# First query tile's loads: heads interleaved over the partitions, list prices and due times changed (attention and two MLPs, Trainium2)

## The chip, the cores and the metric

The kernel runs on one core of one Trainium2 chip. The metric is device time in microseconds of that core, median of the runs shown. The profiled execution is one run of its own, with a profile beside it.

## The reference

```python
def _attn_ref(q, k, v):              # (4, 8, 576, 64): batch, heads, sequence, head size
    scores = scale * np.matmul(q, k.transpose(0, 1, 3, 2))
    mask = block_i >= block_j        # blocks of 64 positions, lower block triangle
    scores = np.where(mask, scores, -1000000000.0)
    scores = scores - np.max(scores, axis=-1, keepdims=True)
    attn = np.exp(scores)
    attn = attn / (np.sum(attn, axis=-1, keepdims=True) + 1e-09)
    return np.matmul(attn, v)

x = attn_out.transpose(0, 2, 1, 3).reshape(B * S, H * D)          # 2304 x 512
h = x @ w_in;   g = s * np.maximum(h, 0) ** 2 + b;  x = g @ w_out   # 512 -> 2048 -> 512
h = x @ w2_in;  g = np.maximum(0.01 * h, h);        x = g @ w2_out  # 512 -> 2048 -> 512
```

All of it is float32. The kernel splits the operands of the large products in two fp32r parts, high and low, and adds three products for each.

## The kernel before

**Tiles.** The sequence is cut in five query tiles of 128 positions (the last has 64), for all four batches at once, so that an MLP block has 512 columns (256 in the last). `ORDER` runs them as 0, 1, 2, 4, 3. The first MLP of a block (`m_in`, lines 967 to 1008, PE line 985; `m_out`, lines 1013 to 1050, PE line 1028) goes over 16 chunks of 128 hidden units, each with 12 matmuls in and 12 out, and the attention of the next tile (`later_block`) is spread between them. The second MLP (PE lines 1235 and 1301) comes after all of it, in six steps of a product with seven terms, one for each quadrant.

**The start.** The first tile has no MLP work to lie beside. For each of four head pairs p (`NP`) it does: loads of keys `fk` and queries `fq`, 64 scores (PE line 647, names s), row maxima on DVE (line 602), exponentials on ACT (line 617), sums and the division on DVE (lines 623 to 632), transposes on PE (line 662, names t) and their copies `pv`, the product with the values (PE line 750, names o), and the split in `xh` and `xl` (lines 563, 565 and 759). Beside that the first chunks of weights are loaded as words (`early`, line 448), decoded on DVE and ACT (lines 408 to 430) and kept as `w`. PE starts with matmuls on zeros (names warm, line 683: `WARM` = 8 and `FILL` = 14), some of them ahead of the scores and some between.

**Layout of the first tile.** A pair has two heads of 64 rows. Before, head 0 lies in partitions 0 to 63 and head 1 in 64 to 127: two loads of keys and three of queries for each pair, each over 64 neighbouring partitions. In `fq` the blocks of the other head must be zero, so that one matmul over 128 partitions gives one head's scores; those blocks are zeroed on DVE and POOL (line 568), and the loads go beside it, to other places. In DRAM the host has laid each pair's rows out in turn (d, head, position), twice.

**What sets the order.** Every instruction group is a `Step` with the engine, its price in us, what it waits for and a due time. `Graph.order()` plays the program by these prices and writes each engine's instructions in the order that comes out; the chip then takes each engine's queue in that order. A transfer's price is the time on the wire from its run length, and a constant to landing (`wire`, `land`, `late`); `rel` is an earliest time. `DUE` moves the due times of single steps by hand, by step number, in tenths of a us. `begin` starts at 30.0 us: the time for which the due times of the first MLP block are set. `LANES = 8`: a load on SP or ACT waits until the eighth load before it has landed.

**The switches between blocks.** At the end of a block its four banks y are copied to `yo` (line 572 on ACT, line 576 on DVE; two buffers `st`), and stored to `yT` (line 1047). A third copy waits until the first store has landed. The next block's first product in a bank (line 1028) waits for that bank's copy.

Of the kernel before, what the change touches and what calls it, by code (L numbers as in the profile page):

```python
# [43 lines left out]
class Graph:  # L44
# [11 lines left out]
    def add(self, eng, fn, after=(), opens=(), uses=(), due=0.0, port=False, nbytes=0, rel=0.0, mode="f", behind=(), run=2048, tail=0.0, wire=None):  # L56
        s = Step(eng, fn, after, opens, uses, due, port, nbytes)
        s.rel = rel
        s.mode = mode
        s.on_pe = "PE" in eng  # L60
        s.tail = tail
        run, into = min(abs(run), 7168), run > 0
        s.wire = nbytes / run * (21.0 + run / 26.4 if into else 3.8 + run / 21.9) / 16e3
        s.land, s.late = 0.82 if into else 0.33, 1.0 if into and not wire else 0.0
        if wire:
            s.wire, s.land = wire
        for p in s.preds:
            p.succs.append(s)
        s.left = len(s.preds)
        for b in s.uses:  # L70
            b.users += 1
            b.left += 1
            if b in s.opens:
                assert b.opener is None
                b.opener = s
            else:
                b.opener.later.append(s)
                s.left += 1
        for g in behind:
            g.later.append(s)  # L80
            s.left += 1
        for g in dict.fromkeys(self.gates[b.key] for b in s.opens if b.key in self.gates):
            g.later.append(s)
            s.left += 1
        self.steps.append(s)
        return s
# [138 lines left out]
def pool(n, two=False):  # L225
# [39 lines left out]
def kernel(  # L265
# [24 lines left out]
    FILL = 14  # L290
    WARM, LATE, PACE, AHEAD = 8, 10, (6.0, 4.9), 3
# [93 lines left out]
    begin, ut, t = [], [], 30.0  # L385
# [55 lines left out]
    def first_weights():  # L441
        for f in range(NF):
# [6 lines left out]
                    [first_done] if f >= LATE else [], [raw] * (i == 0), [raw], (-39.2, -38.7)[i] if f == 0 else due - (30 if f < NF - KEEP else 12), run=4096, nbytes=524288, rel=PACE[0] + PACE[1] * f if f else 0.0)  # L449
# [135 lines left out]
    def softmax(k, banks, cols, P, pcols, due, after, halves=False):  # L585
# [11 lines left out]
        for j, bk, c, n, r in groups:  # L597
# [5 lines left out]
            mx.append(G.add({"DVE": dve(n * r)}, fn, after[j:j + r], [nm] * (j == 0), [nm, bk], due - 4))  # L603
        neg = {}
# [9 lines left out]
        ex = []  # L614
# [64 lines left out]
    for i in range(WARM + FILL):  # L679

        n = 128 if i < WARM else 256
        G.add(
            {"PE": n * 1.67e-3 * (2 if i < WARM else 1)}, lambda e, n=n: e.matmul(out=wb()[:, :n], lhsT=wq()[:, :128], rhs=wq()[:, :n], start=True, stop=True),
# [5 lines left out]
    zeroed = []  # L689
    for i in range(2):  # L690
        e = {"DVE" if i == 0 else "POOL": 1.2}
        a = G.add(e, lambda e, i=i: memz(e, fq[i]()[:64].rearrange("d p b (y c) -> d (p b) y c", c=64)[:, :, 0::3]), opens=[fq[i]], due=-50)
        zeroed.append([a, G.add(e, lambda e, i=i: memz(e, fq[i]()[64:].rearrange("d p b n -> d (p b) n")[:, :, 64:192]), [a], uses=[fq[i]], due=-50)])
    loaded = []
    for p in range(NP):
        due = -40 + 0.5 * p
        ld = []
        for h in range(2):
            r = slice(64 * h, 64 * h + 64)
            q = "ACT" if p == 0 and h or p == 1 and not h else "SP"  # L700
            ld.append(G.add(
                {q: 0.65}, lambda e, p=p, h=h, r=r: e.dma_start(
                    out=fk()[r, p], in_=kT[:, p, r, h, :128].rearrange("b d s -> d b s")),
                [], [fk] if p == 0 and h == 0 else [], [fk], due, run=512, nbytes=131072, wire=(0.47, 1.2),
            ))
            for x, c0, n in (((0, 64, 128),), ((0, 0, 64), (64, 192, 64)))[h]:
                ld.append(G.add(
                    {q: 0.65}, lambda e, p=p, h=h, r=r, x=x, c0=c0, n=n: e.dma_start(
                        out=fq[p // 2]()[r, p % 2, :, c0:c0 + n], in_=qT[:, p, r, h, x:x + n].rearrange("b d c -> d b c")),
                    [], [], [fq[p // 2]], due, run=4 * n, nbytes=1024 * n, wire=(0.47 if n > 64 else 0.33, 1.2),  # L710
                ))
        loaded.append(ld)
    G.add({"ACT": 1.4}, lambda e: e.activation(out=warm, in_=warm, func=ACTF.Exp), [tiny], due=-39.3, behind=[x for ld in loaded[:2] for x in ld if "ACT" in x.eng])
    id_ok = G.add({"SP": 0.65}, lambda e: e.dma_start(out=id_sb, in_=ident), due=-39.1, run=512, nbytes=65536)
    fv_ok = G.add({"SP": 0.65}, lambda e: e.dma_start(out=fv(), in_=v[:, :128].rearrange("b s d -> s b d")), [], [fv], due=-38.3, run=2048, nbytes=1048576)
# [12 lines left out]
    for p in range(NP):  # L728
# [5 lines left out]
        sc = scores(0, [fq[p // 2]], [fk], cols, q_ap, k_ap, [*loaded[p], *zeroed[p // 2]], due, set())  # L734
# [46 lines left out]
    def later_block(blk):  # L781
# [8 lines left out]
        for u in range(NP * B):  # L790
# [5 lines left out]
            if many == 2 or b == 0:  # L796
# [8 lines left out]
                else Q()[rows(h)].rearrange("d (s h c) -> d s h c", h=2, c=64)[:, :ns, h]  # L805
# [4 lines left out]
                    z, [Q] * (flat and h == 0), [Q], due=due - 13, run=(512 if flat else 256), nbytes=32768)  # L810
# [3 lines left out]
            def k_load(e, K=K, b=b, p=p):  # L814
# [7 lines left out]
                    [], [K] * (h == 0), [K], due=due - 13, run=4 * nk, nbytes=256 * nk)  # L822
# [352 lines left out]
    def x_stage(j, key, t):  # L1175
# [4 lines left out]
        def store(r, x, after):  # L1180
            a = x_st[j, r] = G.add({"SP": 0.65}, lambda e: e.dma_start(out=x_dr[j - 1, r - 1], in_=x()), after, [], [x.buf], t + 6, run=-8 * NH, nbytes=1024 * NH)
# [219 lines left out]
```

## Time and profile before

| | us |
|---|---|
| median of 3 runs | 934.68 |
| lowest and highest | 934.17, 935.10 |
| the profiled execution's own time | 935.12 |
| its span | 933.0 |
| PE busy | 919.4 |
| DVE busy | 707.3 |
| ACT busy | 505.1 |

The span is what the profile shows from the first to the last instruction; 2.12 us of the execution lie around it. Busy time of PE counts each matmul from its start to a modelled end, so a full row of PE can still hold short waits. A float32 matmul stands as two passes in the trace.

### The profile page before, as it was taken

What the parts mean: (1) busy time and instruction counts of PE and PEld (TensorE: products, weight loads), DVE (VectorE), ACT (ScalarE), POOL (GpSimd) and SP (SyncE); (2) the same over time, 40 slices, a digit from 0 to 9 for tenths busy, and PEclk for the clock granted to TensorE, in tenths of its full rate; (3) what the DMA queues carried; (4) which work ended last, traced back from release to release, by engine and by line L of the source; (5) the groups of instructions that cost most, each with busy time, mean ns of one, the idle gap of its engine ahead of it and who ended that gap; (6) DMA issues with size and microseconds to landing.
All of it is one profiled execution on the core that took longest, in us unless ns stands there. A gap on an engine that the chain in (4) does not pass through costs nothing.

```text
span 933.0 us, 16316 instructions
## 1 busy us (share of the span) xinstructions
PE 919.4 (99%) x5756; PEld 822.3 (88%) x5756; DVE 707.3 (76%) x1518; ACT 505.1 (54%) x1079; POOL 26.2 (3%) x113
## 2 busy tenths in 40 slices
PE   8999999999999999999999999999999999999998
PEld 7788887777787888888888888999998999999998
DVE  5989888989998667588888764493887748867477
ACT  5887566767677435277666441444554345443342
POOL 1000000000000000000000000000000000000000
PEclk9999999999999999999999999999999999999999
DMA  9996788988878834286329982994349815157212
GB/s 232 329 332 219 265 286 309 367 263 253 286 241 281 286 94 105 67 285 191 103 91 342 409 302 71 419 416 205 102 105 337 315 57 192 52 206 299 79 67 67
DMA packets 117648, 208.22 MB, mean 223 GB/s; under 512 B 20160, under 2 KB 85312, under 8 KB 110912
## 3 DMA queue, kind: packets, MB, share of 16 engines
q1 hardware_dynamic: 116208, 206.67, 64.8%
q8 instruction: 45, 0.74, 0.3%
q10 hardware_dynamic: 1360, 0.52, 0.3%
q14 instruction: 35, 0.29, 0.1%
HBM read 154.47 MB, written 52.69 MB: 222 GB/s over the span
## 4 chain that ended last, share of the span: by engine, by line
PE 89%; DMA 6%; DVE 2%; ACT 1%; issue 1%; SPq 0%; DVEq 0%; ACTq 0%
PE y L1028 20%; PE h L985 19%; PE A L1301 11%; PE A L1235 10%; PE C L1301 5%; PE C L1235 5%; PE o L936 4%; PE t L662 4%; PE s L858 3%; PE B L1301 3%; PE B L1235 3%; DMA yT<-yo 2%; PE s L647 1%; PE s L897 1%; DMA unit<-in_moe_w_in_dram 1%; DMA x_dr<-xs 1%
## 5 line engine op out<-in xcount | busy, mean ns | idle before, releaser
L985 PE MATMUL h<-xh,w 128*128 128x512 f32 (+1 forms) x640 | 211.1, 382 | 0.0
L1028 PE MATMUL y<-gh,w 128*128 128x512 f32 (+1 forms) x640 | 188.6, 378 | 1.6 <-ACT yo L572 1.5
L985 PEld LDWEIGHTS h<-xh,w 128*128 128x128 f32 x640 | 117.8, 188 | 23.4 <-issue 2.3
L1028 PEld LDWEIGHTS y<-gh,w 128*128 128x128 f32 x640 | 112.8, 189 | 21.9 <-ACT yo L572 2.8
L1028 PE MATMUL y<-gl,w 128*128 128x512 f32 (+1 forms) x320 | 118.4, 370 | 0.0
L985 PE MATMUL h<-xl,w 128*128 128x512 f32 (+1 forms) x320 | 118.3, 370 | 0.1
L1235 PE MATMUL A<-xh,wi 128*128 128x384 f32 x384 | 109.7, 335 | 2.1 <-DVE G L1215 2.1
L1113 DVE TENSOR_TENSOR gl<-G,gh 128x384 fp32r<-128x384 f32 x168 | 91.5, 554 | 8.6 <-ACT gh L563 2.8
L1301 PE MATMUL A<-gh,wo 128*128 128x384 f32 x384 | 97.7, 335 | 0.0
L563 ACT ACTIVATE gh<-G 128x384 fp32r<-128x384 f32 x96 | 50.3, 524 | 67.9 <-DVE gl L1113 27.7
L1001 ACT ACTIVATE g<-h 128x512 f32<-128x512 f32 (+1 forms) x80 | 44.2, 552 | 68.2 <-PE h L985 57.8
L1235 PEld LDWEIGHTS A<-xh,wi 128*128 128x128 f32 x384 | 70.4, 188 | 2.5 <-DVE G L1215 2.4
L1249 ACT ACTIVATE G<-G 128x384 f32<-128x384 f32 x72 | 37.7, 525 | 63.0 <-DVE G L1215 63.0
L1028 PEld LDWEIGHTS y<-gl,w 128*128 128x128 f32 x320 | 60.3, 188 | 10.6 <-DVE gl L1004 0.2
L1301 PEld LDWEIGHTS A<-gh,wo 128*128 128x128 f32 x384 | 69.4, 188 | 0.0
L985 PEld LDWEIGHTS h<-xl,w 128*128 128x128 f32 x320 | 60.4, 189 | 8.3 <-DVE xl L759 0.5
L662 PE MATMUL t<-id_sb,p 128*128 128x128 f32 x400 | 64.1, 276 | 0.9 <-DVE p L576 0.6
L1235 PE MATMUL A<-xl,wi 128*128 128x384 f32 x192 | 64.4, 335 | 0.0
L1301 PE MATMUL A<-gl,wo 128*128 128x384 f32 x192 | 64.2, 334 | 0.0
L662 PEld LDWEIGHTS t<-id_sb,p 128*128 128x128 f32 x400 | 47.7, 140 | 17.5 <-issue 4.9
L1113 DVE TENSOR_TENSOR G<-G 128x384 f32<-128x384 f32 x96 | 52.7, 554 | 7.4 <-ACT G L1249 5.9
L1235 PE MATMUL C<-xh,wi 128*128 128x384 f32 x192 | 56.6, 335 | 0.0
(126 smaller groups left out, 1762.8 us busy)
## 6 DMA issues: line engine op xcount, KB each, us to landing
wi<-u_in SPq DMA_DIRECT2D x32, 896.0 KB, 8.5
wo<-u_out SPq DMA_DIRECT2D x28, 1024.0 KB, 7.6
w<-kept SPq DMA_DIRECT2D x16, 1024.0 KB, 9.7
u_in<-unit SPq DMA_DIRECT2D x16, 896.0 KB, 7.2
u_out<-unit SPq DMA_DIRECT2D x16, 896.0 KB, 5.2
early<-in_moe_w_in_dram SPq DMA_DIRECT2D x16, 512.0 KB, 6.6
early<-in_moe_w_out_dram SPq DMA_DIRECT2D x16, 512.0 KB, 7.5
kept<-w SPq DMA_DIRECT2D x8, 1024.0 KB, 8.0
```

What stands on the lines that cost most here:

```text
L563: e.activation(out=out, in_=in_, func=ACTF.Copy)
L647: e.matmul(out=bk()[:, c:c + n], lhsT=q_ap(j), rhs=k_ap(j, n), start=True, stop=True)
L662: e.transpose(tb()[:, x * 128:(x + 1) * 128], P()[:, pc:pc + 128], id_sb)
L858: e.matmul(out=o[h][:, :nk], lhsT=qs()[r, qc], rhs=kk()[r, :nk], start=(n == 0), stop=(n == 2))
L936: e.matmul(out=o()[64 * h:64 * h + 64, n * x:n * x + n], lhsT=V()[:, j, 64 * h:64 * h + 64], rhs=r, start=(j == 0), stop=(j == nj - 1),)
L985: e.matmul(out=h()[:, :T], lhsT=w()[:, wi, c * 128:(c + 1) * 128], rhs=x[blk, c]()[:, :T], start=(c == 0 and n == 0), stop=(c == KD - 1 an ...
L1001: a = G.add({"ACT": act(T)}, lambda e: e.activation(out=g()[:, :T], in_=h()[:, :T], func=ACTF.Relu), [prev], [g], [h], due)
L1028: e.matmul(out=y()[:, :W], lhsT=w()[:, wi, d * 128:(d + 1) * 128], rhs=x()[:, :W], start=(pos == 0 and n == 0), stop=(pos == NF - 1 and n ...
L1113: e.tensor_tensor(out=out, in0=x, in1=y, op=ALU.subtract)
L1235: e.matmul(out=x()[:, :NH], lhsT=in_w[n, i, s]()[:, ai, c], rhs=y()[:, c], start=(first and c == 0 and m == 0), stop=(c == 1 and m == 2), ...
L1249: {"ACT": act(NH)}, lambda e, y=y: e.activation(out=y(), in_=y(), func=ACTF.Prelu, alpha=0.01), [a], [], [y], d2 + 2)
L1301: e.matmul(out=z[d]()[:, :NH], lhsT=out_w[n, r]()[:, s, 2 * i + d], rhs=y(), start=(first and i == 0 and m == 0), stop=(i == 3 and m == 2) ...
```

## The change

It lays the first tile's rows out by turns: row d of head h goes to partition 2d + h. One load brings a pair's keys, over all 128 partitions. The three loads of queries stay 64 rows each, now every second partition. Since zeros and data now share the partitions' rows, the whole of `fq` is zeroed first, one half tile for each pair, in turn on DVE and POOL, and a query load waits for its zeros. The list's price of the loads and stores changes: a load to 64 neighbouring partitions has a floor (`half`), stores get the 1.0 us of `late` that loads had, the stores of `x_dr` get 2.0 us more. The warm-up is 8 + 22 matmuls of 128 columns in place of 8 of 128 and 14 of 256. The early weights' times (`PACE`) and `begin` move by some 3 us, and the table `DUE` is new; step numbers move too, since four steps fewer are in the first tile's loads.

```diff
-    def add(self, eng, fn, after=(), opens=(), uses=(), due=0.0, port=False, nbytes=0, rel=0.0, mode="f", behind=(), run=2048, tail=0.0, wire=None):
+    def add(self, eng, fn, after=(), opens=(), uses=(), due=0.0, port=False, nbytes=0, rel=0.0, mode="f", behind=(), run=2048, tail=0.0, wire=None, half=False, more=0.0):
...
         s.wire = nbytes / run * (21.0 + run / 26.4 if into else 3.8 + run / 21.9) / 16e3
-        s.land, s.late = 0.82 if into else 0.33, 1.0 if into and not wire else 0.0
+        if half:
+            s.wire = max(s.wire, nbytes / 217.6e3)
+        s.land, s.late = (0.82 if into else 0.33) + more, 0.0 if wire else 1.0
...
 DUE = {
-    30:-332, 31:-369, 34:-520, 37:-270, 38:-382, 39:-348, 40:-101, 41:-144, 42:-22, 43:-73, 44:-188, 45:-14, 47:131,
...
+    41:-292, 44:-408, 51:165, 53:182, 55:108, 56:245, 113:576, 147:447, 185:472, 192:441, 197:216, 204:-525,
...
-    FILL = 14
-    WARM, LATE, PACE, AHEAD = 8, 10, (6.0, 4.9), 3
+    FILL = 22
+    WARM, LATE, PACE, AHEAD = 8, 10, (3.0, 4.9), 3
...
-    begin, ut, t = [], [], 30.0
+    begin, ut, t = [], [], 26.5
...
-        n = 128 if i < WARM else 256
+        n = 128
...
-    zeroed = []
-    for i in range(2):
-        e = {"DVE" if i == 0 else "POOL": 1.2}
-        a = G.add(e, lambda e, i=i: memz(e, fq[i]()[:64].rearrange("d p b (y c) -> d (p b) y c", c=64)[:, :, 0::3]), opens=[fq[i]], due=-50)
-        zeroed.append([a, G.add(e, lambda e, i=i: memz(e, fq[i]()[64:].rearrange("d p b n -> d (p b) n")[:, :, 64:192]), [a], uses=[fq[i]], due=-50)])
-    loaded = []
+    zeroed, loaded = [], []
+    for p in range(NP):
+        zeroed.append(G.add({("DVE", "POOL")[p % 2]: 0.95}, lambda e, p=p: memz(e, fq[p // 2]()[:, p % 2]), [], [fq[p // 2]] * (p % 2 == 0), [fq[p // 2]], due=-60 + p))
     for p in range(NP):
         due = -40 + 0.5 * p
-        ld = []
-        for h in range(2):
-            r = slice(64 * h, 64 * h + 64)
-            q = "ACT" if p == 0 and h or p == 1 and not h else "SP"
-            ld.append(G.add(
-                {q: 0.65}, lambda e, p=p, h=h, r=r: e.dma_start(
-                    out=fk()[r, p], in_=kT[:, p, r, h, :128].rearrange("b d s -> d b s")),
-                [], [fk] if p == 0 and h == 0 else [], [fk], due, run=512, nbytes=131072, wire=(0.47, 1.2),
+
+        def keys(e, p=p):
+            x = kT[:, p]
+            e.dma_start(out=fk()[:, p], in_=bass.AP(x.tensor, x.offset, [[S, 128], [kT.ap[0][0], B], [1, 128]]))
+
+        ld = [G.add({"SP": 0.65}, keys, [], [fk] * (p == 0), [fk], due, nbytes=262144, wire=(1.0, 1.2), rel=(0.0, 2.3, 3.5, 5.0)[p])]
+        for h, x, c0, n in ((0, 0, 64, 128), (1, 0, 0, 64), (1, 64, 192, 64)):
+            ld.append(G.add(
+                {"ACT" if p < 2 and (c0 > 0) == (p > 0) else "SP": 0.65}, lambda e, p=p, h=h, x=x, c0=c0, n=n: e.dma_start(
+                    out=fq[p // 2]()[h:127 + h:2, p % 2, :, c0:c0 + n], in_=qT[:, p, :D, h, x:x + n].rearrange("b d c -> d b c")),
+                [zeroed[p]], [], [fq[p // 2]], due + 0.1, nbytes=1024 * n, wire=(0.5 if n > 64 else 0.35, 1.2),
             ))
...
-            a = x_st[j, r] = G.add({"SP": 0.65}, lambda e: e.dma_start(out=x_dr[j - 1, r - 1], in_=x()), after, [], [x.buf], t + 6, run=-8 * NH, nbytes=1024 * NH)
+            a = x_st[j, r] = G.add({"SP": 0.65}, lambda e: e.dma_start(out=x_dr[j - 1, r - 1], in_=x()), after, [], [x.buf], t + 6, run=-8 * NH, nbytes=1024 * NH, more=2.0)
```

In the order that comes out, the change shows first on SP's queue at the program's start. Here `fk` and `fq` are the first tile's keys and queries, `early` is a chunk of weights, `k` and `q` the next tile's, `id_sb` the identity, `fv` the values. Before:

```order
L702 DMA fk<-in_k_dram 64x4x128
L708 DMA fq<-in_q_dram 64x4x64
L708 DMA fq<-in_q_dram 64x4x128
L708 DMA fq<-in_q_dram 64x4x64
L702 DMA fk<-in_k_dram 64x4x128
L714 DMA id_sb<-in_ident_dram 128x128
L448 DMA early<-in_moe_w_in_dram 128x1024
L708 DMA fq<-in_q_dram 64x4x64
L708 DMA fq<-in_q_dram 64x4x128
L702 DMA fk<-in_k_dram 64x4x128
L708 DMA fq<-in_q_dram 64x4x64
L702 DMA fk<-in_k_dram 64x4x128 x2
```

Now:

```order
L700 DMA fk<-in_k_dram 128x4x128
L814 DMA k<-in_k_dram 128x1x256
L705 DMA fq<-in_q_dram 64x4x64 x2
L705 DMA fq<-in_q_dram 64x4x128
L700 DMA fk<-in_k_dram 128x4x128
L451 DMA early<-in_moe_w_in_dram 128x1024
L700 DMA fk<-in_k_dram 128x4x128
L705 DMA fq<-in_q_dram 64x4x128
L705 DMA fq<-in_q_dram 64x4x64 x2
L700 DMA fk<-in_k_dram 128x4x128
L705 DMA fq<-in_q_dram 64x4x64
L711 DMA id_sb<-in_ident_dram 128x128
```

Two more query loads follow there, then `fv` and the second half of the first `early`. The last query load is the 16th transfer on SP now and was the 18th; the one key load for the next tile has moved to the second place, and the identity from the sixth to the fourteenth. ACT issues three query loads now and issued two of keys and three of queries.

On PE, at the program's start (warm: matmuls on zeros; s: scores; t: transposes), before:

```order
L683 MATMUL warm<-wq 128x128 x8
L683 MATMUL warm<-wq 128x256 x3
L647 MATMUL s<-fk,fq 128x64 x4
L647 MATMUL s<-fk,fq 128x128 x4
L683 MATMUL warm<-wq 128x256
L647 MATMUL s<-fk,fq 128x64 x4
L647 MATMUL s<-fk,fq 128x128 x4
L683 MATMUL warm<-wq 128x256 x6
L647 MATMUL s<-fk,fq 128x128 x3
```

Now:

```order
L686 MATMUL warm<-wq 128x128 x18
L650 MATMUL s<-fk,fq 128x64 x4
L650 MATMUL s<-fk,fq 128x128 x4
L650 MATMUL s<-fk,fq 128x64 x4
L650 MATMUL s<-fk,fq 128x128 x4
L686 MATMUL warm<-wq 128x128 x5
L650 MATMUL s<-fk,fq 128x64 x4
L650 MATMUL s<-fk,fq 128x128 x4
L686 MATMUL warm<-wq 128x128 x2
L665 MATMUL t<-id_sb,p 128x128 x8
```

Eighteen warm matmuls of 128 columns stand ahead of the first score, in place of eight of 128 and three of 256, and the first pair's transposes now stand ahead of the fourth pair's scores.

The third place is the first switch between blocks (tile 0 to tile 1). Before, the copies `yo` of three of the four banks stood on ACT like this (the fourth on DVE):

```order
L1001 ACTIVATE g_1768<-h_1683 128x512
L997 ACTIVATE g_1768<-g_1768 128x512
L563 ACTIVATE gh_1783<-g_1768 128x512
L572 ACTIVATE yo_1790<-y_561,s_sb_136 128x512
L572 ACTIVATE pv_329<-t_1778 128x512
L572 ACTIVATE yo_1812<-y_553,s_sb_136 128x512
L1001 ACTIVATE g_1818<-h_1786 128x512
L572 ACTIVATE yo_1838<-y_569,s_sb_136 128x512
```

Now one stands on ACT and three on DVE; the last two of them there:

```order
L533 TENSOR_TENSOR unit_1649<-unit_1649 128x256
L579 TENSOR_SCALAR yo_1840<-y_576,s_sb_136 128x512
L870 TENSOR_SCALAR l_1823<-l_1823 128x2
L533 TENSOR_TENSOR unit_1649<-unit_1649 128x256
L872 RECIPROCAL l_1823<-l_1823 128x2
L579 TENSOR_SCALAR p_1822<-p_1822,l_1823 128x384
L996 TENSOR_TENSOR g_1849<-g_1849,h_1797 128x512
L568 CAST gh_1870<-g_1849 128x512
L1001 TENSOR_TENSOR gl_1879<-g_1849,gh_1870 128x512
L579 TENSOR_SCALAR yo_1886<-y_557,s_sb_136 128x512
```

Before, the three copies on ACT stood two rows apart; now the three on DVE stand eleven and eight rows apart.

## Rows read from the trace of the kernel before

**Rows 1.** The page: the span.
```profile
span 933.0 us, 16316 instructions
```

**Rows 2.** Busy time by stretch: start:end, length, busy us and instructions, granted clock, DMA.
```profile
28.20:60.00 31.80, 31.61 (x173) 25.86 (x172) 29.97 (x57) 24.81 (x47) 2.05 (x7) 1.00 0.95 353
130.00:200.00 70.00, 69.08 (x400) 53.87 (x400) 62.45 (x144) 49.09 (x102) 0.00 (x0) 1.00 0.90 300
900.00:933.00 33.00, 29.10 (x168) 28.77 (x166) 25.38 (x54) 11.00 (x21) 0.00 (x0) 1.00 0.17 48
```

**Rows 3.** Waits of PE: waiting for, us in total, times, longest.
```profile
PE A L1235 <- DVE G L1215: 2.1, 1, 2.1
PE y L1028 <- ACT yo L572: 1.5, 2, 0.9
...
PE s L647 <- DMA fq<-in_q_dram: 1.0, 1, 1.0
```

**Rows 4.** Timeline of PE: start, us, instruction, count, idle before.
```profile
1.31 5.33 PE L683 MATMUL warm<-wq 128*128 128x128 f32 x22 [1.31 <-POOL wq L568]
6.49 2.02 PE L647 MATMUL s<-fk,fq 128*128 128x64 f32 x16
...
8.78 1.95 PE L647 MATMUL s<-fk,fq 128*128 128x64 f32 x16
...
14.76 2.02 PE L647 MATMUL s<-fk,fq 128*128 128x128 f32 x16 [1.44 <-DVE w L430]
...
19.53 1.35 PE L647 MATMUL s<-fk,fq 128*128 128x64 f32 x10 [1.02 <-DMA fq<-in_q_dram]
...
36.14 0.59 PE L985 MATMUL h<-xh,w 128*128 128x512 f32 x1
```

**Rows 5.** The chain that ended last, first 37 us: start, us, what.
```profile
13.42 5.97 DMA fq<-in_q_dram
...
19.53 1.35 PE s L647 x10
```

**Rows 6.** Busy time by stretch again, four of 2 us; columns PE, PEld, DVE, ACT, POOL.
```profile
6.00:8.00 2.00, 2.00 (x16) 1.75 (x16) 0.40 (x1) 0.02 (x1) 0.00 (x0) 1.00 1.31 214
16.00:18.00 2.00, 2.00 (x14) 1.84 (x14) 1.45 (x6) 0.69 (x1) 0.00 (x0) 1.00 1.19 188
18.00:20.00 2.00, 0.98 (x8) 0.61 (x6) 1.65 (x5) 1.45 (x10) 0.00 (x0) 1.00 1.05 303
20.00:22.00 2.00, 1.99 (x18) 1.80 (x17) 0.76 (x2) 0.83 (x4) 0.00 (x0) 1.00 1.06 411
```

**Rows 7.** Transfers: queue, count, KB each, median us to landing.
```profile
yT<-yo SPq DMA_DIRECT2D x16, 256.0 KB, 3.6
...
k<-in_k_dram SPq DMA_DIRECT2D x48, 128.0 KB, 3.8
...
fk<-in_k_dram SPq DMA_DIRECT2D x6, 128.0 KB, 5.5
```

**Rows 8.** Timeline of SP's queue: start, us, transfers issued.
```profile
0.74 0.77 SPq L702 DMA_DIRECT2D fk<-in_k_dram  x1
...
11.46 1.26 SPq L708 DMA_DIRECT2D fq<-in_q_dram  x2
```

**Rows 9.** Busy time by stretch: first row maximum to second-chunk weights; exponentials, first to last.
```profile
7.60:34.87 27.27, 23.37 (x189) 19.73 (x189) 22.16 (x51) 19.80 (x78) 0.30 (x2) 1.00 1.08 321
8.33:26.26 17.93, 14.62 (x110) 12.66 (x109) 13.23 (x34) 13.21 (x68) 0.30 (x2) 1.00 1.10 293
```

**Rows 10.** Groups by form, first 37 us: count, busy us, mean ns.
```profile
L683 PE MATMUL warm<-wq 128*128 128x256 f32 x28 | 7.0, 391 | 0.0
L683 PE MATMUL warm<-wq 128*128 128x128 f32 x16 | 3.8, 431 | 1.3 <-POOL wq L568 1.3
...
L414 DVE SCALAR_TENSOR_TENSOR early<-early 128x1024 int32<-128x1024 int32 x2 | 2.4, 1222 | 0.0
```

**Rows 11.** Timeline of all engines: a zeroing at the start, and the first switch.
```profile
1.04 0.91 DVE L568 MEMSET fq<- 64x1024 f32 x1 [0.18 <-issue]
...
156.63 0.69 ACT L572 ACTIVATE yo<-y,s_sb 128x512 f32<-128x512 f32 x1 [1.79 <-DMA yT<-yo]
...
160.29 0.69 ACT L572 ACTIVATE yo<-y,s_sb 128x512 f32<-128x512 f32 x1 [2.48 <-DMA yT<-yo]
```

More of the change, by code (lines that the diff above doesn't have):

```diff
@@ L448, in first_weights @@
                     {"SP": 0.65}, lambda e, raw=raw, f=f, i=i: e.dma_start(out=raw()[:, i], in_=words(0, f, i)),
-                    [first_done] if f >= LATE else [], [raw] * (i == 0), [raw], (-39.2, -38.7)[i] if f == 0 else due - (30 if f < NF - KEEP else 12), run=4096, nbytes=524288, rel=PACE[0] + PACE[1] * f if f else 0.0)
+                    [first_done] if f >= LATE else [], [raw] * (i == 0), [raw], (-39.2, -38.7)[i] if f == 0 else due - (30 if f < NF - KEEP else 12), run=4096, nbytes=524288, rel=PACE[0] + PACE[1] * f if f else (4.0, 6.0)[i])
                 for i in range(2)
@@ L603, in softmax @@
             mx.append(G.add({"DVE": dve(n * r)}, fn, after[j:j + r], [nm] * (j == 0), [nm, bk], due - 4))
+        ex = []
         neg = {}
@@ L613, in softmax @@
                 neg[j] = a
-        ex = []
         for j, (bk, c, n) in enumerate(cols):
@@ L679 @@
     for i in range(WARM + FILL):
-        n = 128 if i < WARM else 256
+        n = 128
         G.add(
-            {"PE": n * 1.67e-3 * (2 if i < WARM else 1)}, lambda e, n=n: e.matmul(out=wb()[:, :n], lhsT=wq()[:, :128], rhs=wq()[:, :n], start=True, stop=True),
+            {"PE": n * 1.67e-3 * (2 if i < WARM else 1.3)}, lambda e, n=n: e.matmul(out=wb()[:, :n], lhsT=wq()[:, :128], rhs=wq()[:, :n], start=True, stop=True),
             [wq_ok], [wb] * (i == 0), [wb, wq], -90 if i < WARM else 60,
@@ L701 @@
+        for h, x, c0, n in ((0, 0, 64, 128), (1, 0, 0, 64), (1, 64, 192, 64)):
             ld.append(G.add(
-                {q: 0.65}, lambda e, p=p, h=h, r=r: e.dma_start(
-                    out=fk()[r, p], in_=kT[:, p, r, h, :128].rearrange("b d s -> d b s")),
-                [], [fk] if p == 0 and h == 0 else [], [fk], due, run=512, nbytes=131072, wire=(0.47, 1.2),
-            ))
-            for x, c0, n in (((0, 64, 128),), ((0, 0, 64), (64, 192, 64)))[h]:
-                ld.append(G.add(
[L708 to L711, printed above, removed]
+                {"ACT" if p < 2 and (c0 > 0) == (p > 0) else "SP": 0.65}, lambda e, p=p, h=h, x=x, c0=c0, n=n: e.dma_start(
+                    out=fq[p // 2]()[h:127 + h:2, p % 2, :, c0:c0 + n], in_=qT[:, p, :D, h, x:x + n].rearrange("b d c -> d b c")),
+                [zeroed[p]], [], [fq[p // 2]], due + 0.1, nbytes=1024 * n, wire=(0.5 if n > 64 else 0.35, 1.2),
+            ))
@@ L712 @@
         loaded.append(ld)
     G.add({"ACT": 1.4}, lambda e: e.activation(out=warm, in_=warm, func=ACTF.Exp), [tiny], due=-39.3, behind=[x for ld in loaded[:2] for x in ld if "ACT" in x.eng])
-    id_ok = G.add({"SP": 0.65}, lambda e: e.dma_start(out=id_sb, in_=ident), due=-39.1, run=512, nbytes=65536)
-    fv_ok = G.add({"SP": 0.65}, lambda e: e.dma_start(out=fv(), in_=v[:, :128].rearrange("b s d -> s b d")), [], [fv], due=-38.3, run=2048, nbytes=1048576)
+    id_ok = G.add({"SP": 0.65}, lambda e: e.dma_start(out=id_sb, in_=ident), due=-39.1, run=512, nbytes=65536, rel=3.0)
@@ L716 @@
+    fv_ok = G.add({"SP": 0.65}, lambda e: e.dma_start(out=fv(), in_=v[:, :128].rearrange("b s d -> s b d")), [], [fv], due=-38.3, run=2048, nbytes=1048576, rel=8.0)
     sb_ok = [
@@ L733 @@
         k_ap = lambda j, n, p=p: fk()[:, p, j % B, :n]
-        sc = scores(0, [fq[p // 2]], [fk], cols, q_ap, k_ap, [*loaded[p], *zeroed[p // 2]], due, set())
+        sc = scores(0, [fq[p // 2]], [fk], cols, q_ap, k_ap, loaded[p], due, set())
         P = buf("p", [128, 1024], F32) if p < 2 else Buf("spare", lambda p=p: spare()[:, p - 2])
@@ L809, in later_block @@
                     out=q_to(h), in_=qT[b, p, 64 * h:64 * h + 64, h, 128 * k:128 * k + NQ[k]].rearrange("d (s c) -> d s c", c=64)),
-                    z, [Q] * (flat and h == 0), [Q], due=due - 13, run=(512 if flat else 256), nbytes=32768)
+                    z, [Q] * (flat and h == 0), [Q], due=due - 13, run=(512 if flat else 256), nbytes=32768, half=flat)
                 for h in range(2)
@@ L821, in later_block @@
                     out=K()[64 * h:64 * h + 64, :nk], in_=kT[b, p, 64 * h:64 * h + 64, h, :nk]),
-                    [], [K] * (h == 0), [K], due=due - 13, run=4 * nk, nbytes=256 * nk)
+                    [], [K] * (h == 0), [K], due=due - 13, run=4 * nk, nbytes=256 * nk, half=True)
                 for h in range(2)
```

55 rows, old and new, of the table DUE are left out of this document.

## The prediction

> **What bounds the kernel now.** I read the page first, then busy time by stretch, the waits of PE, PE's timeline of the first 37 us, the chain of waits, the transfers, and the same start by engine. The span is 933.0 us [rows 1]. From the point where the first MLP has begun, PE is nearly always busy: 31.61 of 31.80 us in the next stretch, 69.08 of 70 later [rows 2], and the waits named after the start are few, 2.1 us for G in the second MLP and 1.5 us in two waits for a copy `yo` [rows 3]. The last 3.9 us without PE are the last copies and stores [rows 2], which nothing here touches. So a us that the steady part begins earlier is a us off the end, and only three things can move the time: the start, those waits, and new ones.
>
> The start: PE begins the scores of the four head pairs at 6.49, then (second pair, right behind) at 8.8, 14.76 and 19.53 [rows 4]. The third and fourth pairs are late because of loads: the chain goes through a query load that is issued at 13.42 and lands 5.97 us later, into the scores of the fourth pair at 19.53 [rows 5]. The transfer engines are full in that time but move little: 214 GB/s at 6 to 8 us, 188 at 16 to 18, against 411 at 20 to 22, all with a busy share over 1 [rows 6]. In the slow stretches most of what moves is the first tile's loads to 64 neighbouring partitions; in the fast one those have landed. Behind the late scores everything piles up: from the first row maximum to the weights of the second chunk DVE is busy 22.2 of 27.3 us and idle 5.1; from the first exponential to the last ACT is busy 13.2 of 17.9 [rows 9]. The second chunk's matmuls begin at 36.14 [rows 4], 1.27 us after its weights, which are ready at 34.87 [rows 9].
>
> **The change, part by part.**
>
> *The loads.* Twenty loads become sixteen. SP issues one in 0.63 us (two in 1.26) [rows 8], so four fewer are 2.5 us of issue; the key load moved to second place gives 0.6 back. The last query load is 16th on SP: 0.74 + 15 x 0.63 = 10.2 us, or up to 11.5 with waits for the eighth load before it, where it is now issued at 13.42. It lands 3.8 us later, as the next tile's key loads of 128 KB over all partitions do, or 5.5, as the present loads of 128 KB to 64 partitions do [rows 7]: 14.0 to 17.0 us, against 19.4 now. I take about 14.5, since the traffic around it gets lighter. What the 2.1 MB of keys and queries cost on the wire: at 188 to 214 GB/s 9.8 to 11.2 us, at 411 5.1 us [rows 6]. [...]
>
> *The zeros ahead of the query loads.* One memset takes 0.91 us and the first ends at 1.95 [rows 11] (twice the partitions at the same length; I take the same time). The first query load leaves near 2.0 instead of 1.5. The warm matmuls hide this, below; without that cover it is 0.5 us.
>
> *The warm-up.* Ahead of the first score stand 36 passes of 128 columns. Sixteen of those take 3.8 us now, 0.24 each, and the passes of 256 columns later take 0.25 each [rows 10]: the early ones run at half the pace. I let sixteen run at 0.24 and twenty at half of 0.25: 1.31 + 3.8 + 2.5 = 7.6 us for the first score, 1.1 later than 6.49. Bounds: no delay if all run at the later pace (1.31 + 4.5 = 5.8, before the data), 3.4 us later (9.9) if all run at the early one.
>
> *ACT.* The first exponential goes from 8.33 to about 9.4. With all scores there in time, ACT's 13.2 us of work [rows 9] end at 22.6 instead of 26.26, 3.7 us sooner.
>
> *DVE.* Up to the second chunk's weights it has one 1024-wide decode step more, 1.22 us [rows 10], and some casts given to ACT; I take +0.7, between 0 and 1.2. From 8.7 us (7.6 and the 1.1 that lie between first score and first maximum): 22.2 + 0.7 of work and, I choose, 1.0 of the 5.1 us of idle time left (the first pair still waits for its exponentials) make 32.6, against 34.87. The next tile's four scores, which held PE from 34.87 to 36.14, then lie ahead of the weights in PE's idle time, so the second chunk starts at 32.6 instead of 36.14: **-3.5 us**. Bounds: -1.2 if all warm passes are slow, or if 3.3 us of DVE's idle time stay; -5.6 with no warm-up delay and no idle time (7.6 + 22.9 = 30.5).
>
> *The first switch.* ACT stood 1.79 and 2.48 us behind stores that had not landed, with a copy at the head of its queue [rows 11]; PE lost most of 1.5 us at two switches by it [rows 3]. The list now prices stores 1.0 us longer and puts the copies eleven and eight rows apart instead of two. I take one of the two waits as gone, **-0.9 us**; bounds 0 and -1.5.
>
> *All the rest of the order.* The table is new, so every place may win or lose a little. I take 0; bounds -2.1 (the wait for G goes too [rows 3]) and +3.6 (as much again as the 2.1 and 1.5 there are now). The `half` floors and the 2 us on the stores of `x_dr` act only through this order.
>
> Sum: -4.4 us from the profiled execution's own 935.12 (span 933.0 and 2.1 around it) is 930.7. The median of the runs is 0.44 below that execution, so **930.3 us**.
>
> **The rivals.**
>
> *A store's landing stops DVE (slower).* Three of the first switch's four copies now stand on DVE, which is busy 62.45 of 70 us there, where ACT is busy 49.09 [rows 2]. If they find the store not landed, DVE stands as ACT did, 4.3 us [rows 11], with hardly any slack. At two switches that is 8.6 us, in place of 1.5: 934.68 - 3.5 + 7.1 = 938.3. It decides from 5.4 us of loss on (the 3.5 and two more). Against it: the wider spacing, and a store lands in 3.6 us in the median [rows 7]. 0.11.
>
> *PE's clock falls in the start.* [...] 0.08.
>
> *The loads were not what mattered.* If the interleaved loads land no faster, only the issue time is saved: the fourth pair comes at 17.0 instead of 19.53, and the warm-up takes 1.1 of these 2.5 us back: -1.4, so 933.3. The same comes out if DVE fills up in another order. For it: DVE is busy over 80% of that stretch as it is. 0.16, a third of it below 932.8.
>
> *The waits go too.* With both waits for `yo` and that for G gone and the start at -4: 934.68 - 4.0 - 1.5 - 2.1 = 927.1. 0.19.
>
> **How the numbers follow.** The forecast, 929 to 932.7, has 0.46. What a measurement of this kernel can tell from no change is about 0.2%, 1.9 us: faster is below 932.8, slower above 936.6. Faster: 0.46 + 0.19 + 0.06 = 0.71. Same: 0.10 + 0.08 = 0.18. Slower: 0.11. The range goes from 926.8 (the last rival's 927.1 and a little) to 935.0 (the clock's case); it leaves out the 0.11 above, some 0.07 below and at its edges.
>
> **What would show it.** Right: in the first 20 us more GB/s before 16 us than now; fourth pair's scores near 15 to 16 us; last exponential near 22.6; second chunk near 32.6; at the first switch no ACT or DVE idle over 1 us behind a store. Wrong: the first scores at 9 us or later; a granted clock under 1.00 before 40 us; DVE idle behind `yT`; or a start that is 3.5 us earlier while the end is not, which would mean waits that the new order has made later.

## The result, and the profile after

The changed kernel takes 926.49 us in the median of five runs (925.82 to 926.75), the kernel before 934.68 beside it (933.74 to 935.52). The ratio is 0.9912, 95% interval 0.9898 to 0.9927: 8.2 us faster, by the interval 6.8 to 9.5. A second measurement on another chip gave 0.9921 (0.9902 to 0.9940). The forecast was 930.3 with a range from 926.8 to 935.0: the right side, too small, and 0.3 us outside the range.

The page, and busy time by stretch (start:end, length, busy us of PE, PEld, DVE, ACT, POOL, granted clock, DMA share, GB/s), answer to [rows 1, 2]:

```profile
span 924.6 us, 16314 instructions
...
28.20:60.00 31.80, 31.35 (x141) 25.13 (x140) 28.57 (x42) 24.02 (x39) 1.21 (x4) 1.00 0.98 374
130.00:200.00 70.00, 70.00 (x411) 55.23 (x410) 62.05 (x146) 49.06 (x106) 0.00 (x0) 1.00 0.94 314
```

The span is 8.4 us shorter. PE's waits between 60 and 930 us (waiting for, us in total, times, longest) are now one line, where [rows 3] had the 2.1 us for G and the 1.5 for `yo`:

```profile
PE t L665 <- ACT pv L575: 0.3, 1, 0.3
```

A second trace of the changed kernel has three such lines there, 1.9 us together, 0.6 of it for G; none is for `yo`.

PE's timeline at the start, for [rows 4]:

```profile
1.31 6.54 PE L686 MATMUL warm<-wq 128*128 128x128 f32 x36 [1.31 <-POOL wq L571]
7.68 3.74 PE L650 MATMUL s<-fk,fq 128*128 128x64 f32 x32
...
12.38 1.95 PE L650 MATMUL s<-fk,fq 128*128 128x64 f32 x16
...
15.48 1.95 PE L650 MATMUL s<-fk,fq 128*128 128x64 f32 x16
...
32.25 0.50 PE L982 MATMUL h<-xh,w 128*128 128x512 f32 x1 [0.24 <-ACT g L998]
```

The first scores come 1.2 us later than before, the fourth pair's at 15.48 instead of 19.53, the second chunk at 32.25 instead of 36.14: 3.9 us. The chain of waits through the start (start, us, what) no longer holds a load; it goes from the warm matmuls into the scores, over ACT's exponentials up to 18.95 and then mostly on DVE up to the second chunk's weights:

```profile
1.31 6.54 PE warm L686 x36
7.85 3.57 PE s L650 x32
...
30.76 1.14 DVE early L417
31.90 1.15 DVE w L433
33.05 0.04 issue
33.09 2.58 PE h L982 x10
```

Busy time by stretch, from the first row maximum to those weights, and two stretches of the loads, for [rows 9, 6]:

```profile
8.72:33.04 24.32, 22.72 (x198) 19.52 (x197) 23.24 (x51) 22.21 (x82) 0.92 (x4) 1.00 0.99 326
...
6.00:8.00 2.00, 2.00 (x20) 2.00 (x19) 0.00 (x0) 0.00 (x0) 0.00 (x0) 1.00 0.97 287
8.00:10.00 2.00, 2.00 (x21) 2.00 (x19) 0.92 (x3) 0.55 (x4) 0.00 (x0) 1.00 1.07 344
```

DVE is busy 23.24 of 24.32 us, where it was 22.16 of 27.27.

The rest of the gain lies late. Between the second chunk and the last product of the first MLP the two traces differ by 2.4 us more (542.1 against 539.7; the second trace of the changed kernel has 541.1), in the second MLP by another 2.4 (350.5 against 348.1; 348.9 in the second trace). For the latter, look at what DVE did in the kernel before just ahead of PE's wait for G (DVE's timeline; in brackets the idle time and what ended it), and at the chain there:

```profile
714.49 0.36 DVE L565 CAST gh<-G 128x384 fp32r<-128x384 f32 x1 [0.59 <-ACT G L1249]
717.09 0.96 DVE L1113 TENSOR_TENSOR xs<-xs 128x768 f32<-128x768 f32 x1 [2.24 <-DMA x_dr<-xs]
717.97 0.55 DVE L1215 TENSOR_TENSOR G<-C,G 128x384 f32<-128x384 f32 x1
```

```profile
707.16 9.81 DMA x_dr<-xs
```

G was late because DVE stood 2.24 us on a subtract that overwrites a buffer whose store to `x_dr` took 9.81 us to land. That is the store which the change prices 2 us dearer. After it, the same subtract follows without idle time:

```profile
716.89 0.95 DVE L1110 TENSOR_TENSOR xs<-xs 128x768 f32<-128x768 f32 x1
```

### The profile page after: what moved, and what is told of

It is laid out like the page before. It is cut to its first block, busy times and chain, and to the rows that moved or that the text cites. A ratio compares the mean times of both kernels' runs of the same rounds, so it can differ in the third digit from the quotient of the medians.

```text
span 924.6 us, 16314 instructions
## 1 busy us (share of the span) xinstructions
PE 917.0 (99%) x5772; PEld 822.6 (89%) x5772; DVE 703.9 (76%) x1513; ACT 503.2 (54%) x1084; POOL 25.8 (3%) x113
## 4 chain that ended last, share of the span: by engine, by line
PE 94%; DVE 2%; DMA 2%; ACT 1%; issue 0%; SPq 0%; DVEq 0%; POOL 0%; ACTq 0%; POOLq 0%
PE h L982 21%; PE y L1025 21%; PE A L1298 11%; PE A L1232 11%; PE C L1298 5%; PE C L1232 5%; PE t L665 4%; PE o L933 4%; PE B L1232 3%; PE B L1298 3%; PE s L855 2%; PE s L650 2%; DMA k<-in_k_dram 2%; PE s L894 1%; PE warm L686 1%; DVE early L417 0%
## 5 line engine op out<-in xcount | busy, mean ns | idle before, releaser
L566 ACT ACTIVATE gh<-G 128x384 fp32r<-128x384 f32 x90 | 47.1, 524 | 61.9 <-DVE gl L1110 26.5
```

What stands on the lines that cost most here:

```text
L566: e.activation(out=out, in_=in_, func=ACTF.Copy)
```

## The experiments

Two theories stood at this point. *Start and stores:* the start gives 3.5 to 4 us, and the rest is the waits behind stores, that of G above all. *The order at large:* the new table made many places a little better, and the waits named would have gone over into others. Times are medians, each with the kernel before on the same chip. The edits are shown shortened.

**The store behind the wait for G, and the copies `yo`.** The kernel before, its order written out and two edits made to it:

```diff
+seq = list(G.order())
+# t4: x_stage's last subtract; s4: its store
+to = dve_steps[dve_steps.index(t4) + 8]
+seq.remove(t4); seq.insert(seq.index(to) + 1, t4)   # and s4 behind it
+# per block: stores of copies 1 and 2, issued behind those of copies 3 and 4
+s1.fn = lambda e: e.dma_start(out=yT[rows1, cols], in_=o3()[:, :T])
```

> The kernel before, in its own order, with only the two kinds of waits behind stores taken away. The stores of each block's first two copies yo are issued behind its last two copies and read their buffers, so two of the four banks' rows of the first MLP's output hold the other two's values (left out: those rows); and the one subtract before the third token group, at 717.09 us, stands eight DVE steps later. If these waits were worth what PE shows for them (1.5 and 2.1 us): 930.8 to 931.5 us, and more, down to 929.5, if the small waits that follow them go as well. If PE would lose the time at the next wait anyway: 933.7 to 935 us.

930.70 against 933.99, ratio 0.9966 (0.9953 to 0.9979): 3.2 us, and no wait of PE for G or `yo` is left. The waits were worth what PE shows for them. Then each edit alone, first the subtract:

> The kernel before with one of the two edits of the run that had both: only the subtract at 717.09 us stands eight DVE steps later. The run with both gained about 3.3 us. If the wait of A for G was this store's, as the 2.24 us of idle time ahead of the subtract say: 2.1 us, 931.6 to 932.4 us, and no wait of PE over 1 us between 640 and 780 us. If the gain of the run with both came from the two switches: within 0.5 us of before.

931.64 against 934.31, ratio 0.9970 (0.9958 to 0.9982), 2.8 us by the ratio. Its subtract stands at 716.81 with no idle time ahead:

```profile
716.81 0.95 DVE L1113 TENSOR_TENSOR xs<-xs 128x768 f32<-128x768 f32 x1
```

The second MLP takes 348.3 us in this trace and 348.2 in that of both edits, 350.5 to 350.9 in three traces without it, 348.1 and 348.9 in two of the changed kernel. So 2.2 to 2.6 us come from this one step by the traces. (Of the executions with a mean granted clock of 0.999 or 1.00, 11 here and 12 of the kernel before, the means are 931.1 and 933.4: 2.2. The last section returns to the others.) Then the copies:

> The kernel before with the other of the two edits: only the stores of each block's first two copies yo stand behind its last two copies (two of the four banks' rows of the first MLP's output hold the other two's values). The run with both gained about 3.3 us. If the copies' waits are worth the 1.5 us that PE shows for them: 932.0 to 933.0 us. If PE would wait there anyway, for another reason: 933.5 to 934.7 us.

933.25 against 934.31, ratio 0.9991 (0.9977 to 1.0005). About 1 us, which this run can't tell from none. ACT has no idle time behind `yT` left in it.

**The loads.** One part of the change put into the kernel before:

```diff
-fk()[r, p] <- kT[:, p, r, h, :128]          # two loads a pair
+fk()[:, p] <- all 128 rows of kT[:, p]      # one
-fq()[r, ...]             # r: 64 neighbours
+fq()[h:127 + h:2, ...]   # whole pairs zeroed first
 # order of all other steps as before
```

> The kernel before in its own order of steps with one part of the change: keys and queries interleaved over all partitions, one key load a pair, whole pairs zeroed first; nothing else moves. If the loads alone bring the start's gain: the fourth pair's scores at 14 to 16.5 us instead of 19.53, the second chunk 2.5 to 3.5 us earlier than 36.14, no change in the waits behind stores later, and 931.2 to 932.5 us. If the order and the due times are needed for it: less than 1 us, 933.7 to 935 us.

932.04 against 933.99, ratio 0.9982 (0.9972 to 0.9993): 1.7 us by the ratio. The fourth pair comes at 17.11, later than expected, the second chunk at 33.67, and the 2.5 us behind the store of `x_dr` are still there. So the loads alone bring about half of the start's gain. The other way round, the changed kernel with neighbouring partitions:

```diff
-e.dma_start(out=fk()[:, p], in_=bass.AP(...))
+for h in range(2): e.dma_start(out=fk()[64*h:64*h+64, p], in_=kT[:, p, ...])
-out=fq()[h:127 + h:2, ...]
+out=fq()[64*h:64*h+64, ...]
```

> The changed kernel with one part undone: the first tile's keys and queries go to 64 neighbouring partitions again (two key loads a pair, four issues more), zeros, order, prices and due times stay. If the landing of these loads paces the start: fewer than 280 GB/s between 6 and 12 us, the fourth pair's scores at 17.5 to 20 us instead of 15.48, the second chunk's matmuls 2 to 3.5 us later than 32.25, and 928.5 to 930 us. If what was gained at the start came from the order of the work and the loads only had to be fewer or earlier: the second chunk within 1 us of 32.25 and 926 to 927.3 us.

928.83 against 933.99, ratio 0.9950 (0.9936 to 0.9963): about 2 us given back. In the trace, which is of the slowest of its five executions (930.44), the third pair's scores wait 1.58 us for `fq`, the fourth pair comes at 18.12 and the second chunk at 34.70, 2.5 us later. This undid two things at once, the partitions and the number of loads. They are parted by this edit:

```diff
-e.dma_start(out=fk()[:, p], in_=bass.AP(...))
+for h in range(2): e.dma_start(out=fk()[h:127 + h:2, p], in_=kT[:, p, ...])
```

> The changed kernel with its keys in two loads a pair again (twenty loads as before), but both interleaved over every second partition. It parts two things that the run with neighbouring partitions undid together: which partitions a load writes, and how many loads there are. That run had the second chunk at 35.2 us and was 2.3 us slower than the changed kernel. If the partitions matter: the second chunk within 1 us of 32.25, 926.3 to 927.5 us. If the four more issues on SP matter: 34 us or later, 928 to 929.3 us.

(The second chunk of the run with neighbouring partitions, called 35.2 there, is at 34.70.) 929.39 against 934.73, ratio 0.9943 (0.9926 to 0.9960): as slow as with neighbouring partitions. Inside the start the partitions do show. Transfers (queue, count, KB each, median us to landing), neighbouring partitions first, then every second one:

```profile
fk<-in_k_dram SPq DMA_DIRECT2D x8, 128.0 KB, 4.5
```

```profile
fk<-in_k_dram SPq DMA_DIRECT2D x8, 128.0 KB, 3.1
```

The same eight loads land in 3.1 us instead of 4.5, and the first MLP begins at 24.35 instead of 26.21 (23.75 in the changed kernel). That is one trace each; in two others with such loads to neighbouring partitions, six on SP in each, the median is 5.5 us (before) and 4.2 (new prices). Between 6 and 12 us the transfers move 227 GB/s with neighbouring partitions, 243 with every second, and 300 in the changed kernel (means of three stretches of 2 us), so most of that difference comes with the four fewer issues. SP is late by its four more issues, and the next tile's last two query loads, at 20.63 in the changed kernel, leave at 22.99. Timeline of this run, first SP's queue:

```profile
22.99 1.86 SPq L805 DMA_DIRECT2D q<-in_q_dram  x2
```

and then PE:

```profile
30.67 0.56 PE L650 MATMUL s<-k,q 128*128 128x192 f32 x2 [1.30 <-issue]
```

PE stands 1.3 us ahead of the next tile's first score, and the second chunk begins at 34.05. The trace names no releaser there; that it is those two loads is read from their place (they are the last that the score needs, and land in 7.1 us in the median) and was not tried by itself. In the run with neighbouring partitions they leave at 23.75, and the score begins at 31.32 without such a wait, since the first MLP began later. So what shows in the time is the number of issues on SP. Where the rows land shows in the landing times and in the beginning of the first MLP, and with twenty loads not in the time. Sixteen loads to neighbouring partitions were not run.

**The warm matmuls.** The changed kernel with 13 ahead of the first score instead of 18, and one without the 22 behind:

```diff
+for s in warm_steps[1:6]: s.fn = lambda e: None     # first run
+for s in warm_steps[18:]: s.fn = lambda e: None     # second run
```

> The changed kernel with 13 warm matmuls ahead of the first score instead of 18 (26 passes instead of 36), the order otherwise the same. The chain of the changed kernel goes through the warm matmuls up to 7.68 us and then through DVE. If they are what the start waits for: first scores at about 6.6 us, the second chunk up to 1 us earlier than 32.25, 925.4 to 926.2 us. If the first pair's loads land only then, or the clock falls without these passes: no change within 0.3 us, or 0.5 to 4 us slower.

927.05 against 934.31, ratio 0.9923 (0.9907 to 0.9939): no gain. The first scores come at 7.05, the second chunk at 32.05. The chain passes through the warm matmuls, but by the third pair's scores the lead is gone (12.28, against 12.38 and 12.06 in two traces of the changed kernel). DVE, busy 23.24 of the 24.32 us there, is the likely reason; that was not tried.

> The changed kernel without the 22 warm matmuls that stand behind the first two pairs' scores; the 18 ahead of them stay. In the run with the old table PE stood still for 2.18 us at 16.8 us, and its granted clock went from 1.00 to 0.71 and 0.50 right behind. If these matmuls are what keeps the clock: a granted clock under 1.00 between 12 and 30 us, scores and transposes twice as long there, the second chunk 1 to 5 us later, 927.5 to 931.5 us. If the kernel's own matmuls are enough: 1.00 throughout, 926 to 927.3 us.

926.76 against 934.73, ratio 0.9914 (0.9895 to 0.9932). The granted clock stays at 1.00 through the start, also where PE is busy for half of the time (busy time by stretch):

```profile
16.00:18.00 2.00, 0.93 (x8) 0.73 (x7) 2.00 (x5) 2.00 (x13) 0.00 (x0) 1.00 1.03 411
18.00:20.00 2.00, 1.46 (x16) 1.32 (x18) 1.77 (x7) 1.69 (x11) 0.15 (x1) 1.00 1.08 392
```

In the median those matmuls are worth nothing that can be measured. But three of the six executions had a mean granted clock of 0.997 or 0.998 and took 927.2 to 927.5 us, the other three 925.2 to 926.4, and none of the changed kernel's eleven executions was under 0.999. So it isn't shown that they are useless.

**Prices and table.** The changed kernel with the old table of due times, its numbers moved to the same steps:

```diff
-DUE = {41: -292, 44: -408, ...}
+DUE = {30: -332, 31: -369, ...}   # old values, numbers from 50 on raised by 4
```

> The changed kernel with the old table of due times (carried over to the new step numbers); loads, prices of loads and stores, pace and warm-up are the new ones. If the prices of the stores by themselves move the copies and subtracts from behind the stores: no idle time over 1 us behind a store on DVE or ACT, the start within 1 us of the changed kernel's, 926 to 928.5 us. If it takes the new table: the start is earlier by some 3 us, but waits of 1 us or more stand elsewhere, 930 to 934 us.

946.38 against 933.99, ratio 1.0120 (1.0098 to 1.0142): outside both expectations. Its PE timeline and busy time by stretch:

```profile
18.95 3.75 PE L622 MATMUL s<-fk,fq 128*128 128x64 f32 x16 [2.18 <-ACT p L592]
```

```profile
16.00:18.00 2.00, 0.76 (x7) 0.57 (x6) 1.10 (x3) 1.52 (x10) 0.00 (x0) 1.00 1.05 405
18.00:20.00 2.00, 1.05 (x5) 1.08 (x6) 0.00 (x0) 2.00 (x13) 0.00 (x0) 0.71 1.02 410
20.00:22.00 2.00, 2.00 (x11) 2.00 (x11) 1.04 (x5) 1.15 (x5) 0.00 (x0) 0.50 1.03 412
```

PE stands still for 2.18 us, the granted clock goes from 1.00 to 0.71 and 0.50, and the fourth pair's 16 score matmuls take 3.75 us instead of 1.95. The second chunk begins at 42.91, 10.7 us later than in the changed kernel; the first MLP loses as much again. (The trace is of the slowest of the six executions; all six had a mean granted clock of 0.996 or less.)

The other half, the kernel before with the new prices of stores alone:

```diff
-s.land, s.late = 0.82 if into else 0.33, 1.0 if into and not wire else 0.0
+s.land, s.late = (0.82 if into else 0.33) + more, 0.0 if wire else 1.0
 # and more=2.0 for the stores of x_dr
```

> The kernel before with the new prices of stores alone: 1 us more for every store's landing, 2 us more for the stores of x_dr; loads, step numbers and table of due times are the old ones. If the planner then moves the steps that stood behind stores, and little else: no idle time over 1 us ahead of the subtract near 717 us, 930.5 to 932.5 us. If the old due times, found with the old prices, no longer fit: waits of 1 us or more elsewhere, 935 to 945 us.

935.46 against 934.73, ratio 1.0001 (0.9983 to 1.0019): no change by the ratio, and by the median just inside the second expectation. The trace is of an execution of 932.83 us. In it the idle time ahead of the subtract is gone, the second MLP takes 348.2 us, and the first MLP is longer. Waits of PE, in this run:

```profile
PE y L1028 <- ACT yo L572: 1.6, 1, 1.6
...
PE h L985 <- DVE g L999: 0.8, 1, 0.8
```

From the second chunk to the last product of the first MLP it takes 544.0 us, against 542.1, 541.5 and 541.3 in three traces in the old order. The waits for `yo` were 1.5 us before, so the two rows name about 0.9 of the 1.9 to 2.7 us; the rest has no name. The other executions differ by the clock: six of the twelve had a mean of 0.998 or less and took 936.9 us in the mean, the other six 933.1. So the price moves the step from behind its store, and what that brings is lost again with the old table, in the first MLP and in executions with a lower clock; how the table does it was not followed further.

**Together.** The kernel before with the loads, the late subtract and the late stores, in its own order, and the changed kernel again:

> The kernel before in its own order with three edits together: the interleaved loads (2.0 us faster by themselves) and the two that take the waits behind stores away (3.3 us together; two of the four banks' rows of the first MLP's output hold the other two's values). If start and stores are separate gains that add: 928.3 to 929.3 us, which leaves some 2 to 3 us of the changed kernel's gain for the rest of its order. If one hides the other: 930 us or more. If they are all there is: 926 to 927 us.

929.40 against 934.31, ratio 0.9946 (0.9930 to 0.9961): 5.0 us. Loads (1.7) and stores (3.2) add.

> The changed kernel as it is, beside the kernel before and the next three on one chip, since its medians and those of the runs so far were taken on several chips. 925.8 to 927.3 us, 7 to 8.2 us below before; the second chunk's matmuls within 0.5 us of 32.25.

926.93 against 934.73, ratio 0.9921 (0.9902 to 0.9940): 7.4 us; second chunk at 31.93. What is left for the rest of the change (order, table, warm-up) is 2.4 to 3.2 us. Part of it is at the start: the second chunk is at 33.67 and 33.89 in the two runs with the loads and the old order, at 31.93 to 32.25 in the new one, so 1.5 to 2. The last us or so is spread over the first MLP (540.7 us in the mean of six traces in the new order, 541.7 in three in the old one; 541.0, 542.6 and 540.7 in the three with the late stores), which is no more than two executions of one kernel differ by; where it comes from stays open. Some 0.9 us of the gain goes with the granted clock (last section). No run was faster than the changed kernel by more than can be measured.

## Why the prediction fell short

*The start: right.* Forecast -3.5; -3.9 in the first two traces, -3.2 by the means of all that there are (last section). The steps held as well: first score at 7.6, measured 7.68; fourth pair at 15 to 16, measured 15.48; DVE's 22.9 us of work and 1.0 of idle time, measured 23.24 and 1.08; clock 1.00. The reason given for the loads was right in part. The forecast saw the issues on SP and the partitions; the issues show in the time, the partitions, with twenty loads, only in the landing. It read 188 to 214 against 411 GB/s as what the partitions may cost; with the same number of loads it was 227 against 243 between 6 and 12 us. And it didn't see that SP's time is also the next tile's. The same eight key loads took 4.5 and 3.1 us to landing, a factor of 1.5; why neighbouring partitions were slower was not shown.

*The first switch: not told apart.* Forecast -0.9; the run for it gave about 1 us with an interval that holds zero.

*"All the rest of the order ... I take 0": this step failed.* Its lower bound was the wait for G, 2.1 us, and that wait went: 2.2 to 2.6 us in the second MLP, 2.8 by the run that moved one step and nothing else. The wait had been read from PE's list as one for DVE, and so as something that a new table may or may not touch. One view further, DVE's own idle time at 717.09 names the store of `x_dr`, and the diff prices just that store 2 us dearer. The text said that those 2 us "act only through this order", and left it there. That run of prices alone shows what this would have been worth knowing: the new price takes that wait away with the old table too, though it doesn't make that kernel faster. With -2.4 in this place the sum is 927.9. The 1.0 to 1.4 us from there to the two measurements, 926.93 and 926.49, are not pinned to a term; the clock's 0.9 us, which no term had, is of that size. The lower end of the range came from the last rival with its start at -4.0, where the bounds of the sum's own terms (-5.6, -1.5, -2.1) reach 925.5; the second measurement lies just inside the range.

*The rivals.* "The waits go too", 927.1, is nearest to what happened, at 0.19: the waits for G and `yo` are gone, and only what those for `yo` were worth is not told apart. No store stopped DVE in the changed kernel. The clock stayed at 1.00 through the first 40 us of its trace. The upper end of the range, 935.0, is the clock's case, and no run shows that term: with the old table the clock fell to 0.50 behind PE's 2.18 us of waiting for ACT in the start, 16 scores took 3.75 us instead of 1.95, and the time was 946.38. "The loads were not what mattered" is half right. With the same number of loads the interleaved ones landed sooner, in 3.1 us against 4.5, and the fourth pair came at 15.48 and not at 17.0, but in the time only the saved issues show for certain. Its remark that DVE is nearly full is right, and agrees with fewer warm matmuls gaining nothing.

## What to carry over

When PE waits for another engine, go on to what that engine waited for: both kinds of waits named after the start ended at a store that had not landed, with the instruction at the head of the engine's queue wanting the store's buffer (2.24 us of idle time on DVE, 1.79 and 2.48 on ACT [rows 11]). Then ask of each number in the diff which of these it moves. A planner's prices and its tuned table belong together: new prices with the old table were worth nothing, and with loads, pace and warm-up changed as well the kernel came out some 12 us slower than the kernel before.

## What the runs showed of the hardware

- The same start wasn't equally fast each time. In five traces whose instructions up to the second chunk are the kernel before's in its order (before, late subtract, late stores, both, new prices), that chunk begins at 36.14, 34.01, 35.61, 36.38 and 34.01. In four traces of the changed kernel's start (twice as it is, and with fewer warm matmuls ahead or behind) it begins at 31.93 to 32.25. By the means, 35.2 and 32.0, the start gives 3.2 us, so 0.7 of the 3.9 us from one pair of traces is luck. Why the old start spreads so was not tried.
- Some stores landed late: 9.81 us for the one above, one of four that SP issued within 4 us, and 7.5 in the median of the 14 to `x_dr`:

```profile
x_dr<-xs SPq DMA_DIRECT2D x14, 384.0 KB, 7.5
```

- Stands of PE were followed by half the clock with the old table and not in the other traces here, and their length alone didn't tell which. With the old table the granted clock fell to 0.50 behind a stand of 2.18 us; between 290 and 340 us, where PE was idle for 1.44 us, its mean was 0.97. Waits of 2.1 and 2.3 us for G (before, late stores), and stands of 1.14 and 1.61 us in the run without the 22 warm matmuls, left it at 1.00.
- The clock also differed between executions of one kernel. Of the 57 of the kernel before that were timed beside the runs, 26 had a mean granted clock of 0.998 or less and took 935.5 us in the mean; the other 31 took 933.5. None of the changed kernel's eleven was under 0.999, which is some 0.9 us of the gain (26 of 57, times 2.0). Where the clock fell is not shown: all kept traces in the old order are at 1.00. The wait for G is a suspect: with it (before, loads alone, late stores) 32 of 81 executions were at 0.998 or less, with the subtract late (late subtract, both, and those with the loads) 1 of 24. It isn't the only one: with the new prices, where it is gone too, 6 of 12 were.
